# fp32r products that read their moving columns as two halves in turn

## The chip, the cores and the metric

The kernel runs on one core of a Trainium2 chip. The metric is the device time of one execution in microseconds, the median of several runs. Engines are named as in the profile: PE is TensorE's matmuls, PEld its weight loads, DVE is VectorE, ACT is ScalarE, POOL is GpSimd, SP issues the DMAs.

## The reference

Two branches work on the same x (2048 tokens, 512 features) and are mixed by a gate. Branch A is attention with 32 query heads of 16 features that share one key and one value head; branch B is a gated feed-forward layer with 1792 hidden features.

```python
q = (x @ wq).reshape(B, S, 32, 16).transpose(0, 2, 1, 3)
k, v = x @ wk, x @ wv
p = softmax(einsum("bhqd,bkd->bhqk", q, k) * 16 ** -0.5)
a = einsum("bhqk,bkd->bhqd", p, v).transpose(0, 2, 1, 3).reshape(B, S, 512) @ wo
b = (sigmoid(x @ w_gate) * (x @ w_up)) @ w_down
g = sigmoid((x * gate_w).sum(-1, keepdims=True))
out = g * a + (1 - g) * b
```

## The kernel before

Tokens come in 4 blocks of 512 (`TB`), features in 4 chunks of 128 (`KC`). x is passed transposed, so that features lie on the partitions and tokens run along a row. A product whose precision matters is made of three fp32r products: each operand is split into a rounded high half and the rest (`split`), and high × high, high × low and low × high are summed in one PSUM bank (`THREE`). A matmul takes a stationary operand of up to 128 columns and streams a moving operand of 512 columns past it into one bank.

The products are these:

- `project` (L849, matmul at L854): 12 matmuls on all 128 rows for one tile of 128 outputs by 512 tokens. `keys` uses it for keys, values and the gate (moving: x), `query` for the queries (moving: x). `query_out` splits the queries again and `store_q` writes them to DRAM; `load_q` brings them back in the layout of the scores.
- `maximum` (L1137, matmul at L1142): scores of 128 queries against 512 keys, of which DVE takes the maximum over the keys (L1144). Moving: the keys `ks`. The maxima go back into two rows of the query tile and are subtracted by the next product.
- `scores` (L1146, matmul at L1151): scores of 128 keys against 512 queries. Moving: the query tile `qs_t`. ACT takes the exponential (L1153) into a tile p.
- `pv` (L1006, matmul at L1009): the exponentials times the values, plain fp32, four heads side by side on four strips of 32 columns. Moving: p. Each call shows as two matmul records.
- `fill` (L1107, matmul at L1116): the feed-forward layer and the output projection. For gate and up (kinds g and u) the weights are stationary and x is moving; for down, and for the output projection (kinds d, a and e), the hidden or attention tile is stationary and the rows of w_down or wo are moving.
- the last unit's output (L1197), plain fp32, moving: the last chunk of wo.

`maximum`, `scores` and `fill` use 64 rows of the array each. Two of them run at the same time, one on rows 0 to 63 and one on rows 64 to 127, into different banks.

The order of everything is written out by hand: `ORDER` (L669) is a string of codes, one for a pair of 64-row products (one hexadecimal digit says what each half does), V for one `pv` group, G for a projection. `plan` plays the string against a model of the engines (`State`) and gives each engine its list of instructions; a bank, a tile and a buffer are given out by that model. Each engine then works through its list in this order and waits on the others by semaphores. The eight banks are shared by all products; a bank comes free when DVE or ACT has read it.

Of the kernel before, what the change touches and what calls it, by code (L numbers as in the profile page):

```python
# [17 lines left out]
S, D, H, DH, F = 2048, 512, 32, 16, 1792  # L18
P = 128
TB = 512  # L20
NB = S // TB
NT = TB // P
KC = D // P
# [68 lines left out]
def tile_at(j, x):  # L92
    return 2 * (j.i % 2) + x
# [632 lines left out]
def tile_kernel(ctx, tc, x_in, wq, wkv, wo, wg, wu, wd, consts_in, out):  # L726
    nc = tc.nc
# [13 lines left out]
    banks = [pp.tile([P, 512], F32, tag=f"bank{i}", name=f"bank{i}") for i in range(8)]  # L741

    f32 = lambda a: a.bitcast(F32)


    def load(src, name):

        raw = wp.tile([P, 2, 512], F32, tag="raw", name=name, bufs=RAW)
        nc.sync.dma_start(raw[:, :src.shape[1], :], src)
        return raw  # L750
# [9 lines left out]
    X, XR = {}, {}  # L760
# [40 lines left out]
    RAWS, WS = {}, {}  # L801

    def load_item(item):
        kind, b, i = item
        name = "r{}{}_{}".format(*item)
        if kind in "gu":
            RAWS[item] = load(cols2((wg if kind == "g" else wu)[i]), name)
        elif kind == "x":
            RAWS[item] = load(rows2(x_in[(b * KC + 2 * i) * P:(b * KC + 2 * i + 2) * P, :]), name)
        elif kind == "e":  # L810

            raw = wp.tile([P, 2, 512], F32, tag="raw", name=name, bufs=RAW)
            for half in HALF:
                nc.sync.dma_start(raw[half], wo[(KC - 1) * P:, :].rearrange("(i p) n -> p i n", p=64))
            RAWS[item] = raw
        else:
            RAWS[item] = load(rows2((wd if kind == "d" else wo)[2 * i * P:(2 * i + 2) * P, :]), name)
# [22 lines left out]
    part = lambda i: slice(i * P, (i + 1) * P)  # L840
# [5 lines left out]
    BY_X = [(0, HH), (0, LH), (0, HL), (1, HH), (1, LH), (2, HH), (2, LH), (1, HL), (3, HH), (3, LH), (2, HL), (3, HL)]  # L846
    BY_W = [(kc, two) for two in THREE for kc in range(KC)]

    def project(ps, w, b, order=BY_W, between=()):  # L849

        for i, (kc, (p, q)) in enumerate(order):
            if i < len(between):
                early(between[i])
            nc.tensor.matmul(ps, w[:, p, part(kc)], X[b, kc][:, q, :], start=i == 0, stop=i == 3 * KC - 1)  # L854


    wkv_c = fp.tile([P, TB], F32, tag="gs", name="wkv_raw", bufs=2)[:, :KC * 33]
# [13 lines left out]
    qs_t = [cp.tile([P, 2, TB], F32R, name=f"qs{i}") for i in range(3)]  # L871
# [4 lines left out]
    def early(n):  # L876

        for _ in range(n):
            nc.tensor.matmul(banks[7][:, :P], v_aug[:, :4, :], v_aug[:, 4:8, :], start=True, stop=True)
# [14 lines left out]
    ks = cp.tile([P, S], F32R, name="ks")  # L894
# [3 lines left out]
    wq_s = []  # L898
# [11 lines left out]
    def keys(b, _, ps):  # L910
        if b == 0:
            project(ps, wkv_s, b, BY_X, EARLY)
        else:
            project(ps, wkv_s, b)
# [26 lines left out]
    QD = {}  # L941

    def query(b, t, ps):
        project(ps, wq_s[t], b)

    def query_out(b, t, ps):
        hi, lo = QD[b, t] = [ap.tile([P, TB], F32R, tag="p", name=f"q{b}_{t}_{i}", bufs=PB) for i in range(2)]
# [154 lines left out]
    def after(one, other):  # L1102

        tc.add_manual_dep(one.ins, other.ins.name, mybir.DependencyInfo(
            mybir.DependencyClass.Sync, mybir.DependencyReason.DATA), reason="a bank's other rows")

    def fill(h, j, x, at, start, stop, i):  # L1107
        c, (p, q) = at // 3, THREE[at % 3]
        half = HALF[h]
        if j.kind in "gu":  # L1110
            l, r = WS[j.key][half, p, part(2 * c + x)], X[j.b, c][half, q, :]
        else:
            c += 2 * FG[j.i // 2][0] if j.kind == "d" else KC - 1 if j.kind == "e" else 0
            l = (HS if j.kind == "d" else OT)[j.b, c][half, p, part(tile_at(j, x))]
            r = WS[j.kind, j.b, 0 if j.kind == "e" else c][half, q, :]
        ins = nc.tensor.matmul(banks[i], l, r, start=start, stop=stop)  # L1116
        if at == 0 and not start:
            after(ins, CROSS.pop((j.key, x)))
        elif at == j.n - 1 and not stop:
            CROSS[j.key, x] = nc.sync.nop()  # L1120
            after(CROSS[j.key, x], ins)
# [15 lines left out]
    def maximum(h, n, i):  # L1137
        s, pr = divmod(n, 2)
        u, n = divmod(s, NC)
        qt, kb = divmod(n, 4) if u else (n % 4, n // 4)  # L1140
        r = HALF[h]
        nc.tensor.matmul(banks[i], qs_t[u % 3][r, pr, part(qt)], ks[r, kb * 512:(kb + 1) * 512],  # L1142
                         start=True, stop=True)
        nc.vector.tensor_reduce(MX[u][:, pr, h, qt, kb:kb + 1], banks[i], axis=AX.X, op=ALU.max)  # L1144

    def scores(h, n, i):  # L1146
        e, pr = divmod(n, 2)
        pr = 1 - pr
        u, c = divmod(e, NC)
        r = HALF[h]  # L1150
        nc.tensor.matmul(banks[i], ks[r, part(c)], qs_t[u % 3][r, pr, :], start=True, stop=True)  # L1151
        p = PT[u, c, 2 * pr + h] = ap.tile([P, 512], F32, tag="p", name=f"p{u}_{c}_{pr}_{h}", bufs=PB)
        nc.scalar.activation(p, banks[i], AF.Exp, scale=0.25)  # L1153

    on_bank = lambda act: lambda *args: act(*args[:-1], banks[args[-1]])
    acts = {
        "load_x": first_x, "x_first": first_hi, "xf": first_lo, "wq_first": wq_hi, "wq": wq_lo, "keys": on_bank(keys),
        "query": on_bank(query), "turn": on_bank(turn), "keys_out": on_bank(keys_out), "query_out": on_bank(query_out),
        "turned": on_bank(turned), "store_q": store_q, "load_q": load_q, "add_sums": add_sums,
        "load": load_item, "w_hi": w_hi, "w": w_split, "x_hi": x_hi, "x": x_lo,  # L1160
        "f": fill, "gate": gate, "gated": gated, "h": h_split, "part": part_of, "add": add_part, "out": send_out,
        "m": maximum, "max_finish": max_finish, "max_split": max_split, "max_square": max_square,
        "send_max": send_max, "place_max": place_max, "s": scores,
        "values": on_bank(pv), "finish": on_bank(finish), "store": store, "sums": sums, "invert": invert, "send_inverse": send_inverse,
        "spread": spread, "divide": divide,
# [10 lines left out]
    ps = rest[3:]  # L1176
# [5 lines left out]
    o = []  # L1182
# [10 lines left out]
    for i in range(2):  # L1193
        for j in range(4):
            for t in (2 * i, 2 * i + 1):
                r, m = HALF[t % 2], slice(32 * j, 32 * j + 32)
                nc.tensor.matmul(ps[t][m, :], o[i][r, m], WS["last"][r], start=True, stop=True)  # L1197
    BL = [BA.pop((NB - 1, t)) for t in range(NT)]
    for t in (1, 0, 2, 3):
        ba, g = BL[t], gsig[:, n0 + t:n0 + t + 1]  # L1200
# [12 lines left out]
    last = {}  # L1213
# [46 lines left out]
```

## Time and profile before

| | |
|---|---|
| median of 3 runs | 1576.18 us (1576.03 to 1576.42) |
| span of the profiled execution | 1573.0 us |
| PE busy | 1564.3 us, 12910 matmuls |
| PEld busy | 1008.8 us |
| DVE busy | 1339.4 us |
| ACT busy | 1232.0 us |
| POOL busy | 803.0 us |
| moved by DMA | 103.43 MB |
| granted PE clock | full, in all 40 slices |

The profile page lists the busy time of each engine, the chain of work that ended last, and the costliest groups of instructions with their count, their busy time, the mean time of one, and the idle time ahead of them. Matmuls overlap in their records, so the price of one is read from the distance between starts in the timeline, not from its duration. Groups by line and windows of time, with the busy time of each engine in them, are further views of the same trace.

### The profile page before, as it was taken

How to read it: one execution, taken by the hardware profiler on the slowest of the kernel's cores; microseconds unless marked ns; L12 is line 12 of the kernel's file. 1: busy time of each engine (PE TensorE's matmuls, PEld its weight loads, DVE VectorE, ACT ScalarE, POOL GpSimd, SP SyncE). 2: the span in 40 equal slices, each digit the busy share in tenths (PEclk: the TensorE clock that was granted, in tenths of full speed). 3: DMA queues.
4: the chain of work that ended last, by engine and by line, in shares of the span. 5: the costliest groups of instructions: out<-in, count | busy, mean ns of one | idle time of the engine just before them, and what ended most of it. 6: DMA issues, size and time to landing. Idle time of an engine off the chain costs nothing.

```text
span 1573.0 us, 33645 instructions
## 1 busy us (share of the span) xinstructions
PE 1564.3 (99%) x12910; PEld 1008.8 (64%) x12910; DVE 1339.4 (85%) x2278; ACT 1232.0 (78%) x2429; POOL 803.0 (51%) x727
## 2 busy tenths in 40 slices
PE   9999999999999999999999999999999999999998
PEld 7776766666656666666666665666665656666653
DVE  7899899988899788889798888898889888888852
ACT  4277878888788787878788787877878878787897
POOL 4253472655574164377475346265658426538351
PEclk9999999999999999999999999999999999999999
DMA  7421120212122121122121212022212212111011
GB/s 255 167 82 51 35 86 16 66 57 87 42 85 61 43 80 53 34 72 62 61 80 54 76 36 86 17 67 67 76 36 87 66 44 80 53 36 56 19 53 48
DMA packets 63220, 103.43 MB, mean 66 GB/s; under 512 B 24546, under 2 KB 25058, under 8 KB 63060
## 3 DMA queue, kind: packets, MB, share of 16 engines
q1 hardware_dynamic: 63060, 101.29, 20.3%
q8 instruction: 101, 1.65, 0.4%
q14 instruction: 59, 0.48, 0.1%
HBM read 79.51 MB, written 21.75 MB: 64 GB/s over the span
## 4 chain that ended last, share of the span: by engine, by line
PE 98%; DVE 1%; DMA 0%; issue 0%; ACT 0%; POOL 0%; SPq 0%; DVEq 0%; POOLq 0%; ACTq 0%
PE bank L1116 32%; PE bank L1009 30%; PE bank L1142 17%; PE bank L1151 16%; PE bank L854 3%; DVE mx L1144 0%; DMA xf<-x_in 0%; DVE x L787 0%; DVE ba L1207 0%; PE bank L926 0%; PE bank L1197 0%; POOL wg L830 0%; DVE q L949 0%; DVEq L1256 0%; ACT x L781 0%
## 5 line engine op out<-in xcount | busy, mean ns | idle before, releaser
L1144 DVE TENSOR_REDUCE mx<-bank 128x1 f32<-128x512 f32 x2048 | 1254.3, 682 | 168.1 <-PE bank L1142 108.3
L1153 ACT ACTIVATE p<-bank 128x512 f32<-128x512 f32 x2048 | 1040.1, 664 | 4.5 <-PE bank L1151 1.4
L1151 PE MATMUL bank<-qs,ks 64*128 64x512 f32 x2048 | 722.8, 398 | 0.0
L1142 PE MATMUL bank<-ks,qs 64*128 64x512 f32 x2048 | 683.8, 405 | 0.0
L1009 PE MATMUL bank<-p,v_aug 128*32 128x512 f32 x4096 | 480.1, 597 | 0.0
L1142 PEld LDWEIGHTS bank<-ks,qs 64*128 64x128 f32 x2048 | 339.8, 184 | 137.6 <-issue 56.1
L1151 PEld LDWEIGHTS bank<-qs,ks 64*128 64x128 f32 x2048 | 359.0, 184 | 91.3 <-ACT p L1153 27.7
L1016 ACT COPY ou<-bank 128x512 f32<-128x512 f32 x205 | 125.1, 610 | 272.5 <-PE bank L1009 122.7
L1023 POOL TENSOR_TENSOR ou<-ou,ou 128x512 f32<-128x512 f32 x174 | 224.0, 1288 | 170.8 <-ACT ou L1016 168.5
L1116 PE MATMUL bank<-wd,hl 64*128 64x512 f32 x1344 | 272.6, 391 | 0.0
L1009 PEld LDWEIGHTS bank<-p,v_aug 128*32 128x32 f32 x4096 | 113.1, 109 | 248.1 <-issue 219.3
L1116 PE MATMUL bank<-x,wu 64*128 64x512 f32 x1344 | 271.0, 390 | 0.4 <-SPq L1120 0.4
L1116 PE MATMUL bank<-x,wg 64*128 64x512 f32 x1344 | 271.2, 391 | 0.0
L1116 PEld LDWEIGHTS bank<-wd,hl 64*128 64x128 f32 x1344 | 199.9, 184 | 20.6 <-issue 2.5
L1116 PEld LDWEIGHTS bank<-x,wu 64*128 64x128 f32 x1344 | 201.1, 184 | 16.4 <-issue 2.5
L1116 PEld LDWEIGHTS bank<-x,wg 64*128 64x128 f32 x1344 | 200.4, 184 | 17.4 <-issue 1.2
L1095 POOL TENSOR_TENSOR ba<-ba,pa_d 128x512 f32<-128x512 f32 x35 | 44.5, 1282 | 93.3 <-ACT pa_d L1092 93.2
L830 POOL CAST wg<-rg 128x1024 fp32r<-128x1024 f32 x27 | 28.0, 1037 | 122.3 <-PE bank L1116 62.6
L830 POOL CAST wu<-ru 128x1024 fp32r<-128x1024 f32 x27 | 28.0, 1039 | 95.1 <-PE bank L1116 82.7
L757 POOL TENSOR_TENSOR wd<-rd,wd 128x512 fp32r<-128x512 f32 x56 | 72.4, 1293 | 4.5
L757 POOL TENSOR_TENSOR hl<-h,hl 128x512 fp32r<-128x512 f32 x56 | 72.0, 1285 | 4.5
L1116 PE MATMUL bank<-wa,o 64*128 64x512 f32 x360 | 70.5, 391 | 0.0
(80 smaller groups left out, 745.5 us busy)
## 6 DMA issues: line engine op xcount, KB each, us to landing
rg<-wg SPq DMA_DIRECT2D x28, 512.0 KB
ru<-wu SPq DMA_DIRECT2D x28, 512.0 KB
rd<-wd SPq DMA_DIRECT2D x28, 512.0 KB
qs<-qd SPq DMA_DIRECT2D x192, 64.0 KB
qd<-q SPq DMA_DIRECT2D x32, 256.0 KB
od<-ou SPq DMA_DIRECT2D x31, 256.0 KB
xf<-x_in SPq DMA_DIRECT2D x16, 256.0 KB
vd<-od SPq DMA_DIRECT2D x32, 128.0 KB
```

What stands on the lines that cost most here:

```text
L757: lo.tensor_tensor(hl[:, 1, :], raw, f32(hl[:, 0, :]), op=ALU.subtract)
L830: nc.gpsimd.tensor_copy(WS[item][:, 0, :], raw)
L854: nc.tensor.matmul(ps, w[:, p, part(kc)], X[b, kc][:, q, :], start=i == 0, stop=i == 3 * KC - 1)
L1009: nc.tensor.matmul(ps[32 * j:32 * j + 32, :], v_aug[:, c, :], PT.pop((u, c, j)), start=start, stop=stop)
L1016: nc.scalar.copy(to, ps)
L1023: nc.gpsimd.tensor_tensor(SUMS[u], SUMS[u], PARTS_OF[u].pop(0), op=ALU.add)
L1095: nc.gpsimd.tensor_tensor(BA[b, t], BA[b, t], PA[b, t].pop(0), op=ALU.add)
L1116: ins = nc.tensor.matmul(banks[i], l, r, start=start, stop=stop)
L1142: nc.tensor.matmul(banks[i], qs_t[u % 3][r, pr, part(qt)], ks[r, kb * 512:(kb + 1) * 512], start=True, stop=True)
L1144: nc.vector.tensor_reduce(MX[u][:, pr, h, qt, kb:kb + 1], banks[i], axis=AX.X, op=ALU.max)
L1151: nc.tensor.matmul(banks[i], ks[r, part(c)], qs_t[u % 3][r, pr, :], start=True, stop=True)
L1153: nc.scalar.activation(p, banks[i], AF.Exp, scale=0.25)
```

## The change

Two helpers describe a row of 512 columns in two ways. `turns` reads the two halves of a row in turn: column 0, 256, 1, 257 and so on. `pairs` goes through a bank in its own order, written as 256 pairs, so that the shapes of the two agree. Every fp32r product takes its moving operand by `turns`, except the queries' (`query` passes `straight=True`). The last unit's fp32 product, which shares wo with them, does too.

What is read as column n now has to stand at another place. So the tokens of x within each block of 512, and the columns of wo and w_down, are stored by `halves` on the host as all even ones and then all odd ones; read in turn they come in their natural order. The queries, whose product is read straight, keep the stored order of the tokens until `maximum` and `scores`. There the stationary slice of `maximum` takes 128 tokens in the stored order, and `scores` reads its moving queries in turn. The keys that `maximum` reads in turn come in another order, over which a maximum is taken.

```diff
+    turns = lambda a: a.rearrange("p (w c) -> p c w", w=2)
+    pairs = lambda a: a.rearrange("p (c w) -> p c w", w=2)
...
-    def project(ps, w, b, order=BY_W, between=()):
+    def project(ps, w, b, order=BY_W, between=(), straight=False):
...
-            nc.tensor.matmul(ps, w[:, p, part(kc)], X[b, kc][:, q, :], start=i == 0, stop=i == 3 * KC - 1)
+            x = X[b, kc][:, q, :]
+            to, x = (ps, x) if straight else (pairs(ps), turns(x))
+            nc.tensor.matmul(to, w[:, p, part(kc)], x, start=i == 0, stop=i == 3 * KC - 1)
...
     def query(b, t, ps):
-        project(ps, wq_s[t], b)
+        project(ps, wq_s[t], b, straight=True)
...
-        ins = nc.tensor.matmul(banks[i], l, r, start=start, stop=stop)
+        ins = nc.tensor.matmul(pairs(banks[i]), l, turns(r), start=start, stop=stop)
...
-        nc.tensor.matmul(banks[i], qs_t[u % 3][r, pr, part(qt)], ks[r, kb * 512:(kb + 1) * 512],
+        nc.tensor.matmul(pairs(banks[i]), qs_t[u % 3][r, pr, part(qt)], turns(ks[r, kb * 512:(kb + 1) * 512]),
                          start=True, stop=True)
...
-        nc.tensor.matmul(banks[i], ks[r, part(c)], qs_t[u % 3][r, pr, :], start=True, stop=True)
+        nc.tensor.matmul(pairs(banks[i]), ks[r, part(c)], turns(qs_t[u % 3][r, pr, :]), start=True, stop=True)
...
-                nc.tensor.matmul(ps[t][m, :], o[i][r, m], WS["last"][r], start=True, stop=True)
+                nc.tensor.matmul(pairs(ps[t][m, :]), o[i][r, m], turns(WS["last"][r]), start=True, stop=True)
...
+    halves = lambda a: c(np.asarray(a).reshape(-1, TB // 2, 2).transpose(0, 2, 1).reshape(-1, TB))
...
-        "x_in": c(np.asarray(A_x)[0].reshape(NB, TB, D).transpose(0, 2, 1).reshape(NB * D, TB)),
+        "x_in": halves(np.asarray(A_x)[0].reshape(NB, TB, D).transpose(0, 2, 1)),
...
-        "wo": c(np.asarray(A_wo)),
+        "wo": halves(A_wo),
...
-        "wd": c(np.asarray(B_w_down)),
+        "wd": halves(B_w_down),
```

## The prediction

> **What bounds the kernel now.** I read the page's busy times first, then the chain that ended last, then the costliest groups, then single stretches of the timeline.
>
> ```profile
> PE 1564.3 (99%) x12910; PEld 1008.8 (64%) x12910; DVE 1339.4 (85%) x2278; ACT 1232.0 (78%) x2429; POOL 803.0 (51%) x727
> PE 98%; DVE 1%; DMA 0%; issue 0%; ACT 0%; POOL 0%; SPq 0%; DVEq 0%; POOLq 0%; ACTq 0%
> PE bank L1116 32%; PE bank L1009 30%; PE bank L1142 17%; PE bank L1151 16%; PE bank L854 3%; DVE mx L1144 0%; DMA xf<-x_in 0%; DVE x L787 0%; DVE ba L1207 0%; PE bank L926 0%; PE bank L1197 0%; POOL wg L830 0%; DVE q L949 0%; DVEq L1256 0%; ACT x L781 0%
> L1151 PE MATMUL bank<-qs,ks 64*128 64x512 f32 x2048 | 722.8, 398 | 0.0
> L1142 PE MATMUL bank<-ks,qs 64*128 64x512 f32 x2048 | 683.8, 405 | 0.0
> L1009 PE MATMUL bank<-p,v_aug 128*32 128x512 f32 x4096 | 480.1, 597 | 0.0
> ...
> L1116 PE MATMUL bank<-wd,hl 64*128 64x512 f32 x1344 | 272.6, 391 | 0.0
> ...
> L1116 PE MATMUL bank<-x,wu 64*128 64x512 f32 x1344 | 271.0, 390 | 0.4 <-SPq L1120 0.4
> L1116 PE MATMUL bank<-x,wg 64*128 64x512 f32 x1344 | 271.2, 391 | 0.0
> ...
> L1116 PE MATMUL bank<-wa,o 64*128 64x512 f32 x360 | 70.5, 391 | 0.0
> ```
>
> TensorE is the chain from end to end. The change touches the lines L1116, L1142 and L1151 (65% of the chain) and a part of L854; L1009, the plain fp32 product with the values, stays as it is. The 64-row products run two at a time, one on the upper and one on the lower rows, so their (2048 + 2048 + 3 × 1344 + 360) / 2 = 4244 pairs are the count that matters. A duration of 391 ns is not the price of one, since they overlap; the price is the pitch from start to start. Three stretches of the timeline give it (start us, us from first start to last end, instruction, count), with a window that counts the matmuls in the first:
>
> ```profile
> 1296.14 0.39 PE L1142 MATMUL bank<-ks,qs 64*128 64x512 f32 x1
> ...
> 1306.53 0.41 PE L1116 MATMUL bank<-x,wg 64*128 64x512 f32 x1
> ```
>
> ```profile
> 1295.90:1306.70 10.80, 10.80 (x94) 9.33 (x94) 10.37 (x18) 10.72 (x23) 2.18 (x2) 1.00 0.13 38
> ```
>
> ```profile
> 9.30 11.05 PE L854 MATMUL bank<-x,wq 128*128 128x512 f32 x48
> ...
> 391.71 1.92 PE L1009 MATMUL bank<-p,v_aug 128*32 128x512 f32 x16
> ...
> 183.22 4.50 PE L1009 MATMUL bank<-p,v_aug 128*32 128x512 f32 x40
> ...
> 20.19 0.38 PE L926 MATMUL bank<-consts,vt 128*128 128x128 f32 x2
> 20.19 0.60 PE L926 MATMUL bank<-consts,vt 128*128 128x128 f32 x4
> ```
>
> The 94 matmuls are 47 pairs; from the second pair's start to the last one's lie 45 steps in 1306.53 - 1296.14 = 10.39 us, **231 ns a pair**. The 48 query products stand (11.05 - 0.39) / 47 = 226.8 ns apart. The plain fp32 products come four at a time on four column strips: 40 against 16 of them is six more quads in 4.50 - 1.92 = 2.58 us, 430 ns a quad. The fp32 transposes with 128 columns cost (0.60 - 0.38) / 2 = 110 ns each. From 128 to 512 columns plain fp32 thus pays (430 - 110) / 384 = 0.833 ns a column and about 3 ns fixed. If fp32r takes a column in half of that, 0.417 ns, 512 columns cost 213.3 + 3 = 216 ns. They cost 231. So **15 ns of each pair is excess**, which the same engine does not show when it takes columns at half that rate. The window's granted clock of 1.00 says that no throttle makes it.
>
> [...]
>
> **The change, part by part.**
>
> *Host layouts.* Tokens of x and columns of wo and wd are stored as even ones, then odd ones. This is done before the launch; loads keep shapes, counts and queues. Cost 0, nothing covers it and nothing is needed. No instruction, wait or semaphore is added, none is moved past a queue, and the stationary loads stay contiguous.
>
> *Output patterns.* The bank is written in the same order as before, only described as 256 pairs. Cost 0 on the writing side; DVE and ACT read the same bank in the same way.
>
> *Moving reads.* 4244 pairs and the 48 wkv products of L854 now take column 0, 256, 1, 257 and so on: two addresses 1 KB apart. The 192 wq products (L854, called with straight) stay contiguous. No row of before shows such a read, so it is bounded from both sides. The lower end: all excess goes, 231 to 216 ns, 4244 × 15 ns = 64 us (the 48 wkv products add under 1 us; at 214 ns, with no fixed part left, it would be 72 us). The upper end: each column costs as much as in the plain fp32 product, 430 ns, 4244 × 199 ns = 845 us, and 48 × 0.2 = 10 us. Between them stands 0. I take the lower end for the pitch. The nearest row that separates causes is L1009: it reads its moving tiles from the same SBUF, 512 contiguous fp32 columns, with a weight load ahead of each, at half the rate, and its excess is nil. With the change each half-row is visited at just that half rate. If the 15 ns is a hold-up of a place that is asked too fast, it should go. That is a choice: the rows also allow that the PE can't alternate for free.
>
> Could the excess be the weight load instead? Then the change does nothing. These rows are the timeline again:
>
> ```profile
> 600.03 0.18 PEld L1151 LDWEIGHTS bank<-qs,ks 64*128 64x128 f32 x1
> ...
> 600.16 0.39 PE L1151 MATMUL bank<-qs,ks 64*128 64x512 f32 x1
> ```
>
> ```profile
> L926 PEld LDWEIGHTS bank<-consts,vt 128*128 128x128 f32 x16 | 1.9, 139 | 0.8 <-issue 0.4
> ```
>
> A product starts 0.13 us after its weight load starts, though that load is recorded as 0.18; and the transposes run at 110 ns with 139 ns weight loads. Weight loads of that length hide well inside a 216 ns pitch, which speaks against it.
>
> *What is late next.* A faster PE runs into its readers. The windows of two neighbouring periods (us; PE, PEld, DVE, ACT, POOL busy with counts; clock; DMA) and DVE's timeline in the second:
>
> ```profile
> 173.06:187.65 14.59, 14.59 (x130) 9.79 (x126) 12.17 (x20) 11.07 (x22) 5.65 (x5) 1.00 0.10 30
> 187.65:202.41 14.76, 14.76 (x128) 10.35 (x124) 14.23 (x24) 12.07 (x24) 12.38 (x12) 1.00 0.35 104
> ```
>
> ```profile
> 188.18 14.51 DVE L1144 TENSOR_REDUCE mx<-bank 128x1 f32<-128x512 f32 x24 [2.42 <-PE bank L1116]
> ```
>
> In the second period DVE runs 24 reductions without a gap, (14.51 - 0.68) / 23 = 601 ns each; there a faster PE gains nothing, because the order of the work is fixed in ORDER and a bank comes free only when its reader has ended. In the first DVE works 12.17 of 14.59 us, and about 2.4 us of slack is there. A period holds some 43 pairs, so it would like to shorten by 43 × 15 = 0.65 us. Over longer stretches the share lies between:
>
> ```profile
> 100.00:400.00 300.00, 300.00 (x2536) 193.66 (x2534) 271.58 (x462) 235.27 (x465) 162.12 (x147) 1.00 0.19 58
> 400.00:700.00 300.00, 300.00 (x2536) 196.27 (x2535) 262.48 (x445) 243.60 (x484) 157.39 (x143) 1.00 0.19 59
> ```
>
> DVE is busy 91% and 87%, and 4% less time would make it 94% and 91%. Some periods are full already, others have room. I give back half, between none and all: 64 × 0.5 = 32 us stays.
>
> *Sum.* The profiled span is 1573.0 us; the median is 1576.18, 3.2 us around it. 1573.0 - 32 + 3.2 = **1544 us**.
>
> **The rivals.**
>
> *No change.* The excess belongs to the product, not to the read: a fixed part of some 13 ns for turning over 128 fp32r weight columns, whichever way the moving columns come. For it: the 226.8 ns of the 48 query products is very regular, with the readers, loads and stores around them varying. Against it: the two weight-load rows above. Time 1576.
>
> [...]
>
> [...]
>
> *All of it kept.* If DVE's full periods catch up in the open ones, 1576 - 64 = 1512, or 1504 at 214 ns.
>
> **How the numbers follow.** Faster reads, with the readers giving back between none and nearly all: 0.56, of which the likeliest value is 1544 and nearly all lies in 1504 to 1570. No change: 0.16. Slower: 0.28, of which the partial price (up to 1640) is 0.09 and a price near the column rate of plain fp32 0.19. The range from 1504 to 1640 leaves out the 0.19. The likeliest case by itself spans 1504 to 1570. A measurement of this kernel tells about 0.2% (3 us) from no change: 0.56 faster, 0.16 within, 0.28 slower.
>
> **What the profile of after would show.** The wkv products of L854 (turned) against the wq products (straight) are a control inside the run: wq should stay at 226.8 ns, wkv should differ by the read alone. If I am right, pairs of L1142, L1151 and L1116 stand 214 to 220 ns apart in stretches where DVE is not full, PE shows waits for DVE's and ACT's release of banks in its place, and DVE's busy share rises to about 87%. L1009 stays at 430 ns a quad. If pairs stay at 226 to 231 ns, the read was not the excess. If they go to 300 ns and over, with DVE's share falling below 80%, each column pays for its own access, and the prediction is wrong in its sign.

## The result and the profile after

| | before | after |
|---|---|---|
| median | 1576.3 us (1576.03 to 1578.13) | 1566.04 us (1564.49 to 1567.49) |
| ratio | | 0.9931, 95% interval 0.9917 to 0.9945 |
| span of the profiled execution | 1573.0 us | 1564.9 us |

The change makes the kernel 0.7% faster, 10 us; in a later measurement beside other kernels the ratio was 0.9929 (0.9912 to 0.9946). The prediction was 1544 us, 32 us faster. The direction was right, the size three times too large.

The page of after: busy times, then the chain that ended last by engine and line, then the groups of the two readers. The line numbers of after are 4 to 6 higher than before: L1148 is the matmul of `maximum` and L1150 its reduction on DVE, L1157 the matmul of `scores` and L1159 its exponential on ACT, L1122 is `fill`, L1015 `pv` and L860 `project`.

```profile
PE 1555.2 (99%) x12910; PEld 983.3 (63%) x12910; DVE 1333.5 (85%) x2278; ACT 1228.4 (78%) x2429; POOL 799.4 (51%) x727
...
PE 95%; POOL 2%; DVE 1%; DMA 1%; issue 0%; SPq 0%; ACT 0%; DVEq 0%; POOLq 0%; ACTq 0%
PE bank L1015 29%; PE bank L1122 27%; PE bank L1157 19%; PE bank L1148 17%; PE bank L860 3%; DVE mx L1150 1%; DMA rg<-wg 0%; POOL ou L1029 0%; POOL wu L835 0%; DMA od<-ou 0%; DMA qs<-md 0%; POOL hl L761 0%; PE bank L1203 0%; POOL wg L835 0%; POOL wu L834 0%
...
L1150 DVE TENSOR_REDUCE mx<-bank 128x1 f32<-128x512 f32 x2048 | 1249.1, 681 | 163.9 <-PE bank L1148 102.0
L1159 ACT ACTIVATE p<-bank 128x512 f32<-128x512 f32 x2048 | 1042.2, 690 | 3.6 <-PE bank L1157 1.8
```

PE is as full as before (99%), which shows nothing: these matmuls overlap (those of L1122 are recorded as 382 ns each and start 216 ns apart), so one that waits can leave no gap in the busy time. The pitch shows it. First the control, the wkv products read in turn against the wq products read straight. In the timeline of after twelve wkv products:

```profile
22.41 2.84 PE L860 MATMUL bank<-x,wkv_s 128*128 128x512 f32 x12
```

The first pitch of these twelve, after another kind of product, is 299 ns by their starts; the other ten are 215 or 216. The wq products keep 226 and 227 in their steady runs. So the read does what I forecast for it, in the very value: 216 ns. The products with the values, which the change leaves alone, take 467.0 us of the span in both kernels.

Now the stretch from which the prediction took its 231 ns. Here it is in after, first by its second and its last pair, then as a window (us; PE, PEld, DVE, ACT, POOL busy with counts; clock; DMA):

```profile
1288.65 0.38 PE L1148 MATMUL bank<-ks,qs 64*128 64x512 f32 x1
1288.65 0.38 PE L1122 MATMUL bank<-x,wu 64*128 64x512 f32 x1
1288.86 0.38 PE L1157 MATMUL bank<-qs,ks 64*128 64x512 f32 x1
...
1298.47 0.48 PE L1148 MATMUL bank<-ks,qs 64*128 64x512 f32 x1
1298.51 0.44 PE L1122 MATMUL bank<-x,wg 64*128 64x512 f32 x1
1298.79 0.38 PE L1148 MATMUL bank<-ks,qs 64*128 64x512 f32 x1
...
1299.00 0.43 PE L1148 MATMUL bank<-ks,qs 64*128 64x512 f32 x1
1299.01 0.43 PE L1122 MATMUL bank<-x,wg 64*128 64x512 f32 x1
```

```profile
1288.40:1299.20 10.80, 10.80 (x94) 8.63 (x94) 10.36 (x18) 10.69 (x23) 2.23 (x2) 1.00 0.13 38
```

Two pairs stand 0.21 us apart, but at the end one waits 0.28 to 0.32 us. All 45 steps take 1299.01 - 1288.65 = 10.36 us; before they took 10.39. The pitch fell and the stretch stayed as long. ACT's timeline says why, in before and in after:

```profile
1295.98 0.59 ACT L1016 COPY ou<-bank 128x512 f32<-128x512 f32 x1 [3.46 <-issue]
1296.46 10.89 ACT L1153 ACTIVATE p<-bank 128x512 f32<-128x512 f32 x22
```

```profile
1288.51 0.59 ACT L1022 COPY ou<-bank 128x512 f32<-128x512 f32 x1 [3.44 <-issue]
1288.99 10.89 ACT L1159 ACTIVATE p<-bank 128x512 f32<-128x512 f32 x22
```

In both kernels ACT makes 22 exponentials without a gap, 10.89 us, after 3.4 us of idleness during the products with the values. This stretch of pairs ends when its exponentials let go of the banks, and ACT was full in it before the change. Summed over the whole trace of before, the stretches of pairs (from the first start of a run of 64-row products to the next other product) take 1031 us, in which ACT is busy 96% and DVE 91% of the time (1021 us in after, with the same shares); in the 467 us of the products with the values ACT is busy 47% and DVE 73%.

Counted over the starts of the whole trace, 6160 of 8084 distances between a pair's start and the next one's on the same rows lie at 215 to 219 ns in after; in before the median is 231. The first distance of each of the 208 stretches, some 337 ns in before and 320 in after, stands in both kernels. Behind it 1384 distances in after are 13 ns or more above 216; their excess comes to 46 us (half of their sum, as both halves of the rows are counted). The waits of the weight loads of `maximum` and `scores`, which stand for the products behind them, have grown, most of all on ACT's side (engine, line waited for: us in total, times, longest), before and after:

```profile
PEld bank L1142 <- ACT p L1153: 31.1, 59, 0.8
PEld bank L1151 <- ACT p L1153: 27.7, 69, 0.8
...
PEld bank L1142 <- DVE mx L1144: 6.2, 11, 0.8
...
PEld bank L1151 <- DVE mx L1144: 3.0, 5, 0.8
```

```profile
PEld bank L1157 <- ACT p L1159: 52.5, 192, 0.8
PEld bank L1148 <- ACT p L1159: 42.9, 121, 0.8
...
PEld bank L1148 <- DVE mx L1150: 8.9, 23, 0.8
...
PEld bank L1157 <- DVE mx L1150: 8.7, 34, 0.8
```

They went from 128 times to 313 on ACT (59 to 95 us), and from 16 to 57 on DVE (9 to 18 us).

### The profile page after: what moved, and what is told of

Read it like the earlier page. It is cut to its first block, busy times and chain, and to the rows that moved or that the text cites. A ratio compares the mean times of both kernels' runs of the same rounds, so it can differ in the third digit from the quotient of the medians.

```text
span 1564.9 us, 33526 instructions
## 1 busy us (share of the span) xinstructions
PE 1555.2 (99%) x12910; PEld 983.3 (63%) x12910; DVE 1333.5 (85%) x2278; ACT 1228.4 (78%) x2429; POOL 799.4 (51%) x727
## 4 chain that ended last, share of the span: by engine, by line
PE 95%; POOL 2%; DVE 1%; DMA 1%; issue 0%; SPq 0%; ACT 0%; DVEq 0%; POOLq 0%; ACTq 0%
PE bank L1015 29%; PE bank L1122 27%; PE bank L1157 19%; PE bank L1148 17%; PE bank L860 3%; DVE mx L1150 1%; DMA rg<-wg 0%; POOL ou L1029 0%; POOL wu L835 0%; DMA od<-ou 0%; DMA qs<-md 0%; POOL hl L761 0%; PE bank L1203 0%; POOL wg L835 0%; POOL wu L834 0%
## 5 line engine op out<-in xcount | busy, mean ns | idle before, releaser
L1150 DVE TENSOR_REDUCE mx<-bank 128x1 f32<-128x512 f32 x2048 | 1249.1, 681 | 163.9 <-PE bank L1148 102.0
L1159 ACT ACTIVATE p<-bank 128x512 f32<-128x512 f32 x2048 | 1042.2, 690 | 3.6 <-PE bank L1157 1.8
L1157 PE MATMUL bank<-qs,ks 64*128 64x512 f32 x2048 | 727.2, 400 | 0.1
L1148 PE MATMUL bank<-ks,qs 64*128 64x512 f32 x2048 | 682.2, 401 | 0.0
L1015 PE MATMUL bank<-p,v_aug 128*32 128x512 f32 x4096 | 480.1, 597 | 0.0
L1157 PEld LDWEIGHTS bank<-qs,ks 64*128 64x128 f32 x2048 | 359.1, 184 | 127.2 <-ACT p L1159 52.5
L1148 PEld LDWEIGHTS bank<-ks,qs 64*128 64x128 f32 x2048 | 341.9, 185 | 148.7 <-issue 57.2
L1122 PE MATMUL bank<-wd,hl 64*128 64x512 f32 x1344 | 267.5, 382 | 0.0
L1122 PE MATMUL bank<-x,wu 64*128 64x512 f32 x1344 | 266.5, 381 | 0.7 <-SPq L1126 0.7
L1122 PE MATMUL bank<-x,wg 64*128 64x512 f32 x1344 | 265.8, 382 | 0.0
L1015 PEld LDWEIGHTS bank<-p,v_aug 128*32 128x32 f32 x4096 | 113.0, 109 | 242.4 <-issue 214.9
L1122 PEld LDWEIGHTS bank<-wd,hl 64*128 64x128 f32 x1344 | 196.4, 185 | 12.3 <-issue 2.5
L1122 PEld LDWEIGHTS bank<-x,wu 64*128 64x128 f32 x1344 | 196.1, 185 | 9.5 <-issue 2.5
L1122 PEld LDWEIGHTS bank<-x,wg 64*128 64x128 f32 x1344 | 195.6, 185 | 10.0 <-issue 2.0
L1122 PE MATMUL bank<-wa,o 64*128 64x512 f32 x360 | 69.0, 381 | 0.2 <-POOL o L760 0.2
```

The source lines that it names most:

```text
L1015: nc.tensor.matmul(ps[32 * j:32 * j + 32, :], v_aug[:, c, :], PT.pop((u, c, j)), start=start, stop=stop)
L1122: ins = nc.tensor.matmul(pairs(banks[i]), l, turns(r), start=start, stop=stop)
L1148: nc.tensor.matmul(pairs(banks[i]), qs_t[u % 3][r, pr, part(qt)], turns(ks[r, kb * 512:(kb + 1) * 512]), start=True, stop=True)
L1157: nc.tensor.matmul(pairs(banks[i]), ks[r, part(c)], turns(qs_t[u % 3][r, pr, :]), start=True, stop=True)
```

## The experiments

The theory: the read gives its gain in full, and the readers of the banks take it back, ACT first. The rivals: DVE alone takes it back, as the prediction had it; or it is lost in something else (POOL's splits, loads, buffers, PE's own switches).

**The readers relieved.** Two edits, each made to the kernel before and to the changed one, and both together. DVE takes the maximum over half of each bank's columns. ACT makes every second exponential on 8 columns only, and the neighbouring head's tile is used in place of the missing one; both leave out a part of the computation.

```diff
-        nc.vector.tensor_reduce(MX[u][:, pr, h, qt, kb:kb + 1], banks[i], axis=AX.X, op=ALU.max)
+        nc.vector.tensor_reduce(MX[u][:, pr, h, qt, kb:kb + 1], banks[i][:, :256], axis=AX.X, op=ALU.max)
...
+        if pr == 0:
+            p = PT[u, c, h] = PT[u, c, 2 + h]
+            nc.scalar.activation(p[:, :8], banks[i][:, :8], AF.Exp, scale=0.25)
+            return
```

> The kernel before with its readers relieved: the maximum is taken over half of the columns of each bank, and the exponential of every second score tile is left to 8 columns (its neighbour's tile stands in for it). Readers can then hardly hold PE. All theories: PE stays the bound, 1545 to 1570 us, since before showed few waits; it is the base for after_both.

> The changed kernel with the same readers relieved. Theory (DVE and ACT took the gain back): 50 to 64 us below before_both, pairs at 216 ns with no class of pairs at 270 to 285 ns. Rival (the gain is lost elsewhere: POOL's splits, loads, buffers or PE itself): about 10 us below before_both, and the late pairs are still there.

> The changed kernel, only the maximum taken over half of the columns. If DVE took the gain back alone: as after_both, about 50 us below 1566. If ACT did: within 5 us of 1566. If both share it: 10 to 30 us below 1566, with the waits that remain on ACT.

> The kernel before, only the maximum taken over half of the columns. Base for after_dve (1563.5 us): by both theories 1560 to 1575 us, so that DVE relief alone leaves the gain of the change at 5 to 12 us.

> The kernel before; the exponential of every second score tile is left to 8 columns, and its neighbour's tile stands in for it. Base for after_act: 1555 to 1575 us.

> The changed kernel with ACT relieved in the same way, DVE as it is. Relieving DVE alone gave 2.6 us, both 57 us. If ACT alone took the gain: 40 us or more below before_act. If both engines stand behind one another, each alone enough to hold PE: within 20 us of before_act, with waits on DVE in place of those on ACT.

| relieved | before | after | gain of the change |
|---|---|---|---|
| nothing | 1576.3 us | 1566.0 us | 10.3 us |
| DVE | 1573.5 | 1563.5 | 10.0 |
| ACT | 1567.5 | 1546.2 | 21.3 |
| both | 1557.8 | 1508.8 | 49.0 |

(Single times but for the first row; runs of one kernel lie within 3 us of each other.) With both readers out of the way the change is worth 49 us, just under the expected 50 to 64. Of these, 48.6 lie in the stretches of pairs (1013.9 us with both relieved in before, 965.3 in after). The late distances are nearly gone: of the 1384, 47 are left, 5 us, and of 529 distances of 270 to 289 ns 2 are left. So at most a few us can be held back by anything else, with POOL's splits and the loads as they were. ACT's edit also halves the number of p tiles, so their buffers were relieved with it; but in after the exponentials had waited only 3.6 us in all before their starts (L1159 above), so these buffers did not hold them.

DVE's relief alone leaves the gain as it was, and the same weight loads of after then wait for ACT all the more, 453 times instead of 313:

```profile
PEld bank L1157 <- ACT p L1159: 67.9, 264, 0.8
...
PEld bank L1148 <- ACT p L1159: 56.2, 189, 0.8
```

ACT's relief alone doubles the gain to 21.3 us, just over the 20 that were expected if the two engines stand behind one another, and what is left is then DVE's. The weight loads of after with ACT relieved (in after these two rows stand at 5.0 and 8.7 us):

```profile
PEld bank L1015 <- DVE mx L1150: 34.6, 103, 0.4
PEld bank L1157 <- DVE mx L1150: 32.5, 139, 0.8
```

The two stand behind one another. ACT holds the pairs first; where it lets go, DVE does. Busy shares of 78% and 85% over the span hide that, as both, ACT above all, idle more during the products with the values (47% and 73% busy in before) than in the stretches of pairs (96% and 91%).

The table also splits the 15 ns. The kernel before gains 18.5 us by the relief alone (1576.3 - 1557.8), 4.4 ns for each of 4244 pairs: part of what I had called the read's excess was already a wait for readers (17 of the 18.5 us lie in the stretches of pairs, 1031.0 to 1013.9). The read's own part is 226.7 - 216 = 11 ns, 4244 × 11 ns = 47 us, and 49 were found.

**The read by itself.** A kernel with one moving tile x and one stationary tile, both fp32r, and runs of 40 products that differ only in the order of the moving columns. It computes nothing of the reference.

```python
halves = x.rearrange("p (w c) -> p c w", w=2)              # 0 256 1 257
quarters = x.rearrange("p (w c) -> p c w", w=4)            # 0 128 256 384 1
apart16 = x.rearrange("p (b w c) -> p b c w", w=2, c=4)    # 0 4 1 5 2 6 3 7 8
apart4 = x.rearrange("p (b w c) -> p b c w", w=2, c=2)     # 0 2 1 3 4
every2 = x.rearrange("p (c w) -> p w c", w=2)              # 0 2 4
twos = x.rearrange("p (w c t) -> p c w t", w=2, t=2)       # 0 1 256 257 2
```

> A kernel of its own: one fp32r tile, one stationary tile of 128 columns, runs of 40 products that differ in the order in which the moving columns are read; it computes nothing of the reference. Theory (a place of SBUF that is asked too fast; two places asked in turn are each asked at half pace): contiguous 227 to 231 ns, halves 216, quarters and eighths 216, two neighbours from each half in turn 216 to 222, 16 and 64 bytes apart 216 only if the two lie in different places, every second column (8 bytes on) no better than 227. With 256 and 384 contiguous columns the excess over 0.417 ns a column shrinks in proportion: 113 and 170 ns. Rival (a fixed turnover of the weights that the two-level pattern happens to hide): 256 and 384 columns keep the whole 11 ns, 121 and 174 ns, and the same contiguous order written in two levels is as fast as halves. [...]

These are windows from the first start of a run to its last, so each holds 39 steps: contiguous, halves, quarters, eighths, every second column, every fourth, two places 64, 16 and 8 bytes apart, two and four neighbours from each half; then contiguous with 256 and 384 columns, and halves with 256.

```profile
19.44:28.28 8.84, 8.84 (x40) 7.32 (x39) 0.00 (x0) 0.00 (x0) 0.00 (x0) 1.00 0.01 2
28.51:36.92 8.41, 8.41 (x40) 7.37 (x39) 0.00 (x0) 0.00 (x0) 0.00 (x0) 1.00 0.00 0
37.14:48.18 11.04, 11.04 (x41) 7.48 (x39) 0.00 (x0) 0.00 (x0) 0.00 (x0) 1.00 0.00 0
48.46:67.44 18.98, 18.98 (x41) 8.13 (x39) 0.00 (x0) 0.00 (x0) 0.00 (x0) 1.00 0.00 1
67.92:85.54 17.62, 17.62 (x40) 8.10 (x39) 0.00 (x0) 0.00 (x0) 0.00 (x0) 1.00 0.00 0
86.00:103.99 17.99, 17.99 (x41) 8.13 (x40) 0.00 (x0) 0.00 (x0) 0.00 (x0) 1.00 0.00 0
104.45:112.88 8.43, 8.43 (x40) 7.39 (x39) 0.00 (x0) 0.00 (x0) 0.00 (x0) 1.00 0.01 2
113.10:121.52 8.42, 8.42 (x41) 7.37 (x39) 0.00 (x0) 0.00 (x0) 0.00 (x0) 1.00 0.00 0
121.73:130.59 8.86, 8.86 (x41) 7.33 (x39) 0.00 (x0) 0.00 (x0) 0.00 (x0) 1.00 0.00 0
130.81:144.06 13.25, 13.25 (x41) 7.70 (x39) 0.00 (x0) 0.00 (x0) 0.00 (x0) 1.00 0.01 1
144.40:154.16 9.76, 9.76 (x40) 7.38 (x39) 0.00 (x0) 0.00 (x0) 0.00 (x0) 1.00 0.00 0
163.52:168.19 4.67, 4.67 (x40) 4.67 (x39) 0.00 (x0) 0.00 (x0) 0.00 (x0) 1.00 0.00 0
168.31:175.08 6.77, 6.77 (x41) 6.77 (x40) 0.00 (x0) 0.00 (x0) 0.00 (x0) 1.00 0.01 2
175.25:179.60 4.35, 4.35 (x40) 4.35 (x40) 0.00 (x0) 0.00 (x0) 0.00 (x0) 1.00 0.00 0
```

Divided by 39: contiguous 227 ns, halves 216, quarters 283, eighths 487, every second 452, every fourth 461; 64 and 16 bytes apart 216, 8 bytes apart 227; two neighbours in turn 340, four 250. The contiguous order written in two levels costs 227 as well, but tests nothing: in the trace its operand is one level of 512 columns, like the plain contiguous one. Places 8 bytes apart do keep their two levels and cost 227, so an order in levels is not by itself what helps. Of my expectations halves and the places 64 and 16 bytes apart came true; quarters, eighths and two neighbours, for which I had expected 216 to 222, did not. My theory of a place that is asked too fast falls on two counts. The excess does not shrink with the columns: at 0.417 ns a column (half of plain fp32's 0.833, and within 1% the rise of these rows, (226.7 - 119.7) / 256 = 0.418), 256 and 384 columns should cost 106.7 and 160 ns, and cost 120 and 174, over by the same 13 ns as 512. And quarters, which ask each place still more slowly, are slower.

The distance from one column to the next does not decide the price by itself. Every second column (8 bytes on) costs 452 ns and every fourth (16 bytes on) 461, twice the contiguous pitch, and eighths (256 bytes on) 487; quarters (512 bytes on) cost 283, and halves (1 KB on) and places 16 bytes apart 216, the least of all. No single rule that covers these rows came out of the runs. For this change the row of halves decides.

**The weight load.** The fixed 13 ns could be the next product's weight load taking slots of the moving read. A second kernel of the same sort varies the stationary tile.

> A kernel of its own, as the first one with read orders; it computes nothing of the reference. The first one showed the excess of a contiguous read to be fixed (13 ns over 0.417 ns a column at 256, 384 and 512 columns), which took away the theory of a pace that is too fast. Theory now (the next product's weight load takes read slots from the moving columns, and halves in turn leave it slots): with 64 and 32 stationary columns the contiguous pitch falls to about 221 and 218 ns; with stationary columns taken from every fourth place it rises to 250 ns or more, and halves in turn then cost more than 216 too. Rival (a fixed start of a contiguous fp32r read, whatever the weights are): 227 ns with 128, 64, 32 and spread stationary columns alike, 216 with halves. Plain fp32: 429 ns contiguous; halves in turn the same by both.

Its windows, again 39 steps each: stationary columns contiguous; from every fourth place; the same with halves; then 64 columns contiguous and halves, 32 columns contiguous and halves. Between them stands plain fp32, contiguous and halves, with 79 steps.

```profile
20.34:29.18 8.84, 8.84 (x40) 7.32 (x39) 0.00 (x0) 0.00 (x0) 0.00 (x0) 1.00 0.01 2
29.41:38.58 9.17, 9.17 (x40) 9.17 (x40) 0.00 (x0) 0.00 (x0) 0.00 (x0) 1.00 0.00 0
38.81:48.10 9.29, 9.29 (x40) 9.29 (x40) 0.00 (x0) 0.00 (x0) 0.00 (x0) 1.00 0.00 0
66.51:100.41 33.90, 33.90 (x80) 15.01 (x79) 0.00 (x0) 0.00 (x0) 0.00 (x0) 1.00 0.00 0
100.84:143.50 42.66, 42.66 (x81) 15.01 (x79) 0.00 (x0) 0.00 (x0) 0.00 (x0) 1.00 0.00 0
150.54:159.51 8.97, 8.97 (x40) 5.23 (x39) 0.00 (x0) 0.00 (x0) 0.00 (x0) 1.00 0.00 0
159.74:168.16 8.42, 8.42 (x41) 5.30 (x40) 0.00 (x0) 0.00 (x0) 0.00 (x0) 1.00 0.00 0
168.37:177.41 9.04, 9.04 (x41) 4.25 (x40) 0.00 (x0) 0.00 (x0) 0.00 (x0) 1.00 0.00 0
177.63:186.05 8.42, 8.42 (x40) 4.25 (x39) 0.00 (x0) 0.00 (x0) 0.00 (x0) 1.00 0.01 2
```

With 64 and 32 stationary columns a contiguous product costs 230 and 232 ns, not less than with 128, and halves 216 with each. By their starts, contiguous stationary columns taken from x itself and two stationary tiles in turn leave the contiguous product at 227. So the size of the weight load does not make the excess; the rival, a fixed cost of a contiguous fp32r read, is what is left, and it was not tested further. A spread stationary tile does cost: 235 ns contiguous, 238 with halves, less than the 250 of the theory and more than the 227 of the rival. The two orders are alike there and PEld is busy throughout, so the weight load is probably the bound; this was not tested. Plain fp32 goes from 429 ns a record (two to a product) to 540 with halves, which I had not expected: of the two types the trick helps fp32r alone. The change also turns the one plain fp32 product at the end (L1203); its groups there stand about 110 ns further apart, some 0.3 us in all.

**A new order for the new pitch.** If the readers' place in the order takes the gain, another order should return some. The kernel's own model of the engines charges 100 units for a pair. With 93 units (216 ns at the 2.33 ns a unit that its total and the span of before give) and waits where a bank is not yet free, it gives the old order 1565 us, the span that was measured. A search by moves of single codes brought it to 1558 in that model.

```diff
-            self.now += 100
+            self.now += 93
...
 ORDER = (
...
```

> The changed kernel once more, beside the next two: 1566 us, 0.7% below the kernel before.

> The changed kernel with the order of the work searched anew, by moves of single codes, in the kernel's own model of the engines with 93 units for a pair in place of 100 (a pair's new pitch); the same instructions in another order. If what is lost of the gain hangs on where the order puts the readers' work: about 6 us below the changed kernel, since the model, which gives the old order 1565 us at 93 units, gives the new one 1558. If the readers' waits come back wherever they are moved: within 2 us of the changed kernel.

> The same new order with contiguous reads. If the new order only pays with the faster read: 1575 us or more, no better than the kernel before. If it is simply a better order: 5 us or more below 1576.

| | median | ratio to before |
|---|---|---|
| changed kernel again | 1564.41 us (1563.91 to 1566.03) | 0.9929 (0.9912 to 0.9946) |
| the same with the new order | 1564.12 us (1563.69 to 1564.43) | 0.9926 (0.9911 to 0.994) |
| new order, contiguous reads | 1592.15 us | single time |

A miss: the 6 us of the model do not exist on the chip. Waits for ACT fell in number, from 313 to 281, but hardly in time (95 to 94 us); those for DVE grew from 57 to 65, 18 to 27 us (weight loads of the new order; L1158 is the reduction, L1167 the exponential there):

```profile
PEld bank L1156 <- ACT p L1167: 52.7, 150, 0.8
...
PEld bank L1165 <- ACT p L1167: 41.2, 131, 0.8
...
PEld bank L1156 <- DVE mx L1158: 18.1, 36, 0.8
...
PEld bank L1165 <- DVE mx L1158: 8.9, 29, 0.8
```

With contiguous reads this order is 16 us slower than the kernel before (1575.9 us beside it), so it leans on the faster read and still gets nothing from it. Whether a search over larger moves, or a model with finer costs, would do better stays open.

## Why the prediction was right or wrong

- **The read: right, to the nanosecond.** 216 ns a pair instead of 226 to 231, with L860's wkv at 216 and its wq at 227 as the control.
- **The reason for it: wrong.** I put the excess down to a place that is asked too fast and argued by the plain fp32 product. The excess is fixed per product (13 ns at 256, 384 and 512 columns), and plain fp32 gets slower by the same trick (540 ns instead of 429). That an fp32r column costs half of a plain fp32 one was assumed; the 0.418 ns measured between 256 and 512 columns bear it out. The choice came out right by luck, as quarters or twos would have had the same argument and cost 283 and 340 ns.
- **The term of 64 us: too large.** 15 ns × 4244 took all of 231 - 216 for the read. By the relieved kernels 11 ns are the read's (49 us found) and 4 ns were already waits for readers (18.5 us).
- **"I give back half": the step that failed.** Of 49 us 10 stayed; 39, four fifths, were given back. I weighed DVE alone, between its full periods and its mean shares of 91% and 87%, and chose the middle; for ACT I put down nothing. The row that held the answer stood in the prediction: in the window of 10.80 us from which I took the pitch ACT is busy for 10.72. I read its count of matmuls and its clock, and not that column. Over all stretches of pairs ACT was busy 96% of the time, in before as in after.
- **What is late next:** worked out for DVE's release of banks alone, with ACT's named once and without a number. It is ACT's first (95 us of waits of the weight loads in after, 18 on DVE), with DVE close behind it.
- **Slower, at 0.28: not this order.** No run shows the partial price (up to 1640 us), or a price near the column rate of plain fp32, for two halves in turn; the runs showed 216 ns in their place. Other orders do cost 452 to 487 ns (every second column, every fourth, eighths in turn).
- **DVE's share rising to 87%:** it stayed at 85%, as the span hardly shrank.

## What to carry to other kernels

Ask what a faster engine gains in the stretch where it is to be faster: take the windows in which its instructions lie and read the busy time of each engine that must empty its results, before and beside any share over the span. Where two readers are both near full, relieving one shows little (here the change is worth 10.0 us with DVE relieved, 21.3 with ACT, 49 with both), so test them alone and together. For fp32r products with the moving row contiguous, reading the row as two alternating halves is worth 11 ns of 227 here, if the layouts allow it and the readers have room; four places in turn cost 283 ns here, eight 487 and every second column 452, so any other order must be measured first.

## What the runs showed of the hardware that was not expected

- An fp32r product costs 13 ns beyond 0.417 ns a column with 256, 384 and 512 contiguous columns (120, 174 and 227 ns). Two places in turn take that to about 2 ns at 512 columns (216), and 5 ns at 256 (112). Why a contiguous read costs this once a product, and two places in turn don't, stays open.
- Two places in turn, 16 bytes, 64 bytes or 1 KB apart, cost 216 ns, and 8 bytes apart 227; four in turn cost 283 ns, eight 487; two neighbours in turn from two places cost 340. Plain fp32 pays 540 instead of 429 ns for two places in turn.
- The pitch of fp32r pairs in the kernel before, 231 ns at the median, was partly its readers' doing: with both relieved its median is 227.
